# Batch 1's load order, the weights' gate, q(3)'s loads and the place of batch 2's attention in a fused attention and feed-forward kernel

## The chip, the cores and the metric

The kernel runs on one core of a Trainium2 chip. The metric is device time in microseconds (us) of one execution. A profile shows one execution under the hardware profiler; its span is 1.9 to 2.7 us shorter than the time of the run that it belongs to, so spans are compared with spans and times with times. PE is TensorE, PEld its loading of weights, ACT is ScalarE, DVE is VectorE, POOL is GpSimd, SP is SyncE. The granted clock is the share of full speed that PE was given, 1.00 or 0.50 in the stretches shown here. A trailing q, as in SPq, marks the issue of a DMA.

## The reference

Eight batches of eight heads, 576 positions of width 64, go through a linear attention. The result, 4608 tokens of width 512, goes through a gated feed-forward layer 512 to 1536 to 512.

```python
def phi(x, c, s):
    r = np.maximum(x, 0.0)
    return np.concatenate([r * c, r * s], axis=-1)
q_p, k_p = phi(q, cos_w, sin_w), phi(k, cos_w, sin_w)
kv  = np.einsum('bhsf,bhsd->bhfd', k_p, v)
z   = np.sum(k_p, axis=2)
num = np.einsum('bhsf,bhfd->bhsd', q_p, kv)
den = np.einsum('bhsf,bhf->bhs', q_p, z)[..., None] + 1e-06
x   = (num / den).transpose(0, 2, 1, 3).reshape(4608, 512)
g   = x @ w_gate
out = (0.5 * g * (1 + erf(g / sqrt(2))) * (x @ w_val)) @ w_out
```

## The kernel before

The 4608 tokens are cut into nine blocks of 512. Block n is multiplied by the gate and value weights in twelve units of eight matmuls (`gv_unit`, 512 columns, 1.73 us each); the second product is cut into parts of four matmuls (`o_part`, 0.86 us). A batch has 576 positions, so the attention of batch n+1 must be done, nearly, when block n+1 starts. It is woven into block n's units. Its steps are: load q, k, v in f32; prepare them in nine slices (`prep`: relu times cosine on DVE, relu times sine on ACT); transpose q (`turn_q`, two DMA transposes on the sync queue); `kv_unit`; five `nm_unit`, each eight small matmuls and a division on DVE; and transpose x (`turn_x` by DMA, `turn_x_pe` on PE with a copy on ACT). The argument takes each engine to run its instructions in the order of the program; two of the experiments below show it at work (ACT stood 2.79 and 7.45 us before sines whose load was late, with other work behind them: with the load order alone, and with q(3)'s loads behind).

The loads and the weights on GpSimd's queue, which the change reorders:

```python
nc.gpsimd.tensor_copy(gate, vx_tiles[0][:, 0, 0, 0:1])   # waits for v(0)'s cast; the weights come after it
load_w(0, 2)
load_w(2, 2)
for part in range(2):
    prep("q", 0, part, (8,), eng=nc.gpsimd)
for jt in (4, 6, 8, 10):
    load_w(jt, 2)
# ... q(1) in two halves
load_wo(0, 4)
# ... k(1) and v(1) in two halves each
load_wo(4, 4)
load_wo(8, 4)
# ... q(2), k(2), v(2), then the casts of v(1)
```

Between block 0 and block 1 stands a list `order`, in which the second product of block 0 (`o`) alternates with batch 1's attention. The loop over the blocks, cut to what the argument touches:

```python
for n in range(1, NB):
    b = n + 1
    t_kv, t_nm, t_q, t_k = {1: (4, 6, 7, 12), 2: (3, 4, 6, 9)}.get(n, (1, 2, 4, 8))
    for jt in range(JT):
        gv_unit(n, jt)
        # ...
        if n == 1 and jt == 0:
            turn_x(1, NT - 1)
            turn_q(b)
            loads(b + 1)              # q(3), k(3), v(3) on the sync queue
        # ...
        if jt == t_kv:
            kv_unit(b)
        # ... turn_x(b, i) for i = jt - t_nm - 1, casts of v
        if 0 <= jt - t_nm < NT:
            nm_unit(b, jt - t_nm)
        if b + 1 < B:
            if 0 <= jt - t_q < 3:
                prep_third("q", b + 1, jt - t_q)
            # ... k(b + 1) from unit t_k
            if jt == min(t_nm + NT, JT - 1):
                turn_q(b + 1)
                if b + 2 < B:
                    loads(b + 2)
```

## Time and profile before

| | before |
|---|---|
| time, median of the first 3 runs | 333.91 us (333.26 to 334.19) |
| span of the profile | 331.6 us |
| PE busy | 317.8 us, 96% |
| ACT, DVE busy | 48%, 51% |

The page of the kernel before gives the busy time of each engine, and then, in 40 slices of the span, the busy share of PE and its granted clock in tenths (9 is 90% or more).

```profile
PE 317.8 (96%) x2360; PEld 161.0 (49%) x2398; DVE 169.1 (51%) x400; ACT 159.8 (48%) x335; POOL 29.0 (9%) x45
...
PE   8799979989999999999999999999999999999995
...
PEclk9999989999999999999999999999999999999999
```

PE is the limit. Apart from the last slice, it has holes only in the first ten slices of 8.3 us, and the clock dips once, in the sixth. So only time before some 86 us can be had.

The view of the waits names the holes. Its columns are: the engine, tile and line that waited, what it waited for, the sum in us, how often, and the longest.

```profile
PE ps L401 <- DMA wo_sb<-in_moe_w_out_dram: 2.3, 1, 2.3
PE ps L281 <- DMA qT<-qp: 1.4, 1, 1.4
```

Line 401 is the second product, line 281 is `nm_unit`. The timeline of the kernel before shows where they stand: start, length, engine, line, operation, tiles, count, and in brackets the idle time before and what ended it.

```profile
44.29 1.03 PE L401 MATMUL ps<-wo_sb,hT 128*128 128x512 bf16 x4
...
47.62 1.86 PE L401 MATMUL ps<-wo_sb,hT 128*128 128x512 bf16 x4 [2.31 <-DMA wo_sb<-in_moe_w_out_dram]
...
60.17 1.02 PE L375 MATMUL ps<-xT,wg_sb 128*128 128x512 bf16 x4
...
63.13 8.26 SPq L192 DMA_TRANSPOSE qT<-qp  x2
...
73.63 0.19 PE L281 MATMUL ps<-kv_sb,qT 128*128 128x65 bf16 x1
...
75.25 0.40 PE L281 MATMUL ps<-kv_sb,qT 128*128 128x65 bf16 x7 [1.42 <-DMA qT<-qp]
```

The line at 60.17 is block 1's first unit. The four matmuls at 47.62 take 1.86 us, where the four at 44.29 take 1.03. The view by windows tells why. Its columns are the window, its length, then busy time and count for PE, PEld, DVE, ACT and POOL, the granted clock, the share of the DMA engines and GB/s.

```profile
44.02:47.44 3.42, 1.29 (x12) 0.66 (x10) 2.36 (x8) 1.64 (x3) 2.05 (x4) 1.00 1.24 212
47.44:50.85 3.41, 3.23 (x11) 1.41 (x11) 0.42 (x1) 0.00 (x0) 1.01 (x1) 0.50 1.08 373
```

PE stood still for 2.3 us, and then had 3.41 us at half clock. Half of that, 1.7 us, is the estimate of what it costs.

Last, the chain of waits that ended last holds two DMAs of this stretch (start, length, what):

```profile
32.07 15.52 DMA wo_sb<-in_moe_w_out_dram
...
66.56 8.64 DMA qT<-qp
```

### The profile page before, as it was taken

How to read it: one execution, taken by the hardware profiler on the slowest of the kernel's cores; microseconds unless marked ns; L12 is line 12 of the kernel's file. 1: busy time of each engine (PE TensorE's matmuls, PEld its weight loads, DVE VectorE, ACT ScalarE, POOL GpSimd, SP SyncE). 2: the span in 40 equal slices, each digit the busy share in tenths (PEclk: the TensorE clock that was granted, in tenths of full speed). 3: DMA queues.
4: the chain of work that ended last, by engine and by line, in shares of the span. 5: the costliest groups of instructions: out<-in, count | busy, mean ns of one | idle time of the engine just before them, and what ended most of it. 6: DMA issues, size and time to landing. Idle time of an engine off the chain costs nothing.

```text
span 331.6 us, 6186 instructions
## 1 busy us (share of the span) xinstructions
PE 317.8 (96%) x2360; PEld 161.0 (49%) x2398; DVE 169.1 (51%) x400; ACT 159.8 (48%) x335; POOL 29.0 (9%) x45
## 2 busy tenths in 40 slices
PE   8799979989999999999999999999999999999995
PEld 3585535545455445544554455445544444444443
DVE  5864654957846854755375537562632322223211
ACT  8764755947654752754365436553232223322220
POOL 1785350200000000000000000000000000000000
PEclk9999989999999999999999999999999999999999
DMA  7999999699599999979957994770321111111123
GB/s 283 215 177 266 299 283 348 133 153 381 93 156 367 160 134 355 219 115 183 389 96 113 198 370 79 126 128 12 79 57 39 44 43 35 32 34 32 32 65 95
DMA packets 67757, 53.23 MB, mean 161 GB/s; under 512 B 44048, under 2 KB 53008, under 8 KB 67728
## 3 DMA queue, kind: packets, MB, share of 16 engines
q1 hardware_dynamic: 57920, 40.91, 52.3%
q0 software_dynamic: 9648, 11.80, 15.8%
q8 instruction: 19, 0.31, 0.4%
q10 hardware_dynamic: 160, 0.13, 0.2%
q14 instruction: 10, 0.08, 0.1%
HBM read 37.75 MB, written 9.44 MB: 142 GB/s over the span
## 4 chain that ended last, share of the span: by engine, by line
PE 78%; DMA 13%; POOL 3%; ACT 2%; issue 1%; DVE 1%; SPq 0%; DVEq 0%
PE ps L375 46%; PE ps L401 26%; DMA wo_sb<-in_moe_w_out_dram 5%; DMA wv_sb<-in_moe_w_val_dram 3%; PE ps L281 3%; DMA qT<-qp 3%; PE ps L240 2%; DMA vf<-in_v_dram 2%; POOL wg_sb L94 1%; POOL wv_sb L95 1%; PE ps L624 1%; POOL qp L161 1%; ACT qp L159 1%; ACT gel L383 1%; ACT kp L159 0%
## 5 line engine op out<-in xcount | busy, mean ns | idle before, releaser
L384 DVE TENSOR_TENSOR hT<-gel,ps 128x512 bf16<-128x512 f32 (+2 forms) x114 | 75.0, 660 | 133.0 <-PE ps L375 131.7
L383 ACT ACTIVATE gel<-ps 128x512 f32<-128x512 f32 (+2 forms) x114 | 65.6, 575 | 112.0 <-PE ps L375 109.9
L375 PE MATMUL ps<-xT,wg_sb 128*128 128x512 bf16 (+2 forms) x451 | 111.5, 368 | 0.5
L375 PE MATMUL ps<-xT,wv_sb 128*128 128x512 bf16 (+2 forms) x445 | 110.5, 368 | 0.4
L401 PE MATMUL ps<-wo_sb,hT 128*128 128x512 bf16 x400 | 104.5, 383 | 3.7 <-DMA wo_sb<-in_moe_w_out_dram 2.3
L375 PEld LDWEIGHTS <-wv_sb 128*128 128x128 bf16 x456 | 44.0, 98 | 49.6 <-DMA wv_sb<-in_moe_w_val_dram 0.3
L375 PEld LDWEIGHTS <-wg_sb 128*128 128x128 bf16 x456 | 43.4, 98 | 47.4 <-issue 0.3
L401 PEld LDWEIGHTS <-hT 128*128 128x128 bf16 x420 | 38.7, 98 | 43.9 <-issue 3.7
L410 ACT COPY o_sb<-ps 128x512 f32<-128x512 f32 x34 | 20.0, 588 | 31.6 <-PE ps L401 30.5
L159 ACT ACTIVATE kp<-kf,sin_t 128x256 bf16<-128x256 f32 (+1 forms) x75 | 30.5, 483 | 0.3 <-DMA kf<-in_k_dram 0.3
L159 ACT ACTIVATE qp<-qf,sin_t 128x256 bf16<-128x256 f32 x70 | 30.4, 502 | 0.5 <-DMA qf<-in_q_dram 0.5
L294 DVE TENSOR_TENSOR x_sb<-ps,rec 128x512 bf16<-128x512 f32 x38 | 26.3, 691 | 1.3
L161 DVE TENSOR_SCALAR qp<-qf,cos_t 128x256 bf16<-128x256 f32 x71 | 22.4, 373 | 0.9 <-DMA qf<-in_q_dram 0.9
L281 PEld LDWEIGHTS <-qT 128*128 128x128 bf16 x304 | 14.5, 98 | 9.1 <-DMA qT<-qp 1.7
L161 DVE TENSOR_SCALAR kp<-kf,cos_t 128x256 bf16<-128x256 f32 x63 | 18.3, 349 | 0.0
L281 PE MATMUL ps<-kv_sb,qT 128*128 128x65 bf16 x304 | 16.1, 194 | 1.5 <-DMA qT<-qp 1.4
L249 ACT CAST kv_sb<-ps 128x260 bf16<-128x260 f32 x14 | 4.6, 382 | 16.1 <-PE ps L240 16.1
L139 PE MATMUL ps<-dummy 128*128 128x512 bf16 x28 | 9.1, 484 | 1.5 <-POOL dummy L113 1.5
L240 PEld LDWEIGHTS <-kp 64*128 64x128 bf16 x504 | 8.5, 95 | 3.1 <-issue 3.1
L178 DVE CAST vx<-vf 128x1152 bf16<-128x1152 f32 x12 | 9.2, 770 | 0.8 <-DMA vf<-in_v_dram 0.8
L240 PE MATMUL ps<-vx,kp 64*128 64x65 bf16 x504 | 9.3, 191 | 0.1
L292 DVE TENSOR_SCALAR den<-ps 128x8 f32<-128x8 f32 x38 | 6.1, 160 | 5.1 <-PE ps L281 5.0
(53 smaller groups left out, 96.1 us busy)
## 6 DMA issues: line engine op xcount, KB each, us to landing
out_dram<-o_sb SPq DMA_DIRECT2D x70, 128.0 KB, 2.6
kf<-in_k_dram SPq DMA_DIRECT2D x12, 576.0 KB, 6.8
vf<-in_v_dram SPq DMA_DIRECT2D x12, 576.0 KB, 8.6
qf<-in_q_dram SPq DMA_DIRECT2D x10, 576.0 KB, 5.1
qf<-in_q_dram POOLq DMA_DIRECT2D x4, 576.0 KB, 12.8
kf<-in_k_dram POOLq DMA_DIRECT2D x4, 576.0 KB, 13.9
vf<-in_v_dram POOLq DMA_DIRECT2D x4, 576.0 KB, 14.2
wg_sb<-in_moe_w_gate_dram POOLq DMA_DIRECT2D x6, 256.0 KB, 6.6
```

Of the source, the lines that this page charges most:

```text
L139: nc.tensor.matmul(bank(to), lhsT=dummy[:, 0:128], rhs=dummy, start=True, stop=True)
L159: nc.scalar.activation(o, i, AF.Relu, scale=tab[:, j:j + 1])
L161: (eng or nc.vector).tensor_scalar(o, i, 0.0, tab[:, j:j + 1], op0=ALU.max, op1=ALU.mult)
L178: copy(vx_tiles[b % 2][:, m0:m1, j0:j1, 0:D], staged["v", b][:, m0:m1, j0 * D:j1 * D].rearrange("p m (j d) -> p m j d", d=D),)
L240: nc.tensor.matmul(bank(6 + i)[:, m * (D + 1):(m + 1) * (D + 1)], lhsT=kp[rr, m, j, :], rhs=vx[rr, m, j, :], start=(j == 0), stop=(j == R ...
L281: nc.tensor.matmul(bank(b0 + h // 4)[:, (h % 4) * (D + 1):(h % 4 + 1) * (D + 1)], lhsT=q_cols(b, t, h), rhs=kv_sb[b][:, h // 2, h % 2, :], ...
L294: nc.vector.tensor_tensor(x, nm[:, :, :, 0:D], rec[:, :, :, None].to_broadcast([128, 2, 4, D]), op=ALU.mult,)
L375: nc.tensor.matmul(bank(b0 + g)[:, 0:w], lhsT=wt[:, ct, js], rhs=xt[:, ct, c0:c0 + w], start=(ct == 0), stop=(ct == CT - 1),)
L383: nc.scalar.activation(gel[:, 0:w], bank(b0)[:, 0:w], AF.Gelu)
L384: nc.vector.tensor_mul(hT[n][:, jt, c0:c0 + w], gel[:, 0:w], bank(b0 + 1)[:, 0:w])
L401: nc.tensor.matmul(bank(to), lhsT=hT[n][:, jt, tt * 128:(tt + 1) * 128], rhs=wo_sb[:, jt, :], start=(jt == 0), stop=(jt == JT - 1),)
L410: copy(o_sb, bank(to))
```

## The change

Its intent is to take those two waits away. The second part of `wo` goes ahead of v(1). The weights wait for an earlier event, so the whole queue runs ahead. q(2) is prepared sooner, piece by piece, between the pieces of batch 1's attention. q(3) loads before q(2)'s transposes, not behind them. Batch 2's attention starts at unit 7 of block 1, not 6, so that q(2) may arrive later. Transposes of x(0,4) go from DMA to PE. The diff, cut to its core (`...` marks cuts; left out are the move of k(2)'s slices by two units in block 1 and the new entries of `order`):

```diff
-    nc.gpsimd.tensor_copy(gate, vx_tiles[0][:, 0, 0, 0:1])
+    nc.gpsimd.tensor_copy(gate, phi["q", 0][:, 0, JA - 1, 0:1])
     load_w(0, 2)
     load_w(2, 2)
-    for part in range(2):
-        prep("q", 0, part, (8,), eng=nc.gpsimd)
     ...
     load_wo(0, 4)
-    for name in ("k", "v"): ... load(nc.gpsimd, name, 1, m, m + 2)
+    for m in (0, 2):
+        load(nc.gpsimd, "k", 1, m, m + 2)
     load_wo(4, 4)
+    for m in (0, 2):
+        load(nc.gpsimd, "v", 1, m, m + 2)
     load_wo(8, 4)
     # q(2), k(2); casts of v(1); and now v(2) behind the casts

     # block 0
+        if jt > 1:
+            prep("q", 0, jt - 2, (R - 1,), eng=nc.scalar)
-        if jt == 6:
-            turn_x(0, 4)
+        if jt == 7:
+            turn_x_pe(0, 4, 5, act_copy)
-        if jt == 10:          # q(1)'s first 16 transposes, now at the head of `order`
-            turn_j(1, 0, 2, range(4), 4, dve_copy)
-            turn_j(1, 2, 4, range(4), 5, act_copy)

     # `order`: q(2)'s slices 0 and 1, then 2, then 3 between the pieces;
     # nm(1, 4) and the transpose of x(1, 3) leave it for block 1
-    prep("q", 2, 0, range(R))
+    for m in (0, 2):
+        load(nc.sync, "q", 3, m, m + 2)

-        t_kv, t_nm, t_q, t_k = {1: (4, 6, 7, 12), 2: (3, 4, 6, 9)}.get(n, (1, 2, 4, 8))
+        t_kv, t_nm, t_q, t_k = {1: (5, 7, 7, 12), 2: (3, 5, 6, 9)}.get(n, (1, 2, 4, 8))
         for jt in range(JT):
-            gv_unit(n, jt)
+            if n > 1 or jt > 1:
+                gv_unit(n, jt)
+            else:
+                for i in range(2):
+                    gv_unit(n, i, jt * HALF, HALF)
+                    j = JA + 2 * jt + i
+                    prep("q", b, 1, (j,), eng=nc.scalar)
+                    prep("q", b, 0, (j,))
+                    if jt == i == 0:
+                        turn_x_pe(1, 3, 5, act_copy)
-                if n == 1 and jt == 0:
+                if n == 1 and jt == 2:
+                    prep("q", b, 0, (R - 1,))
+                    prep("q", b, 1, (R - 1,), eng=nc.scalar)
+                    turn_q(b)
+                    nm_unit(1, NT - 1)
+                if n == 1 and jt == 3:
                     turn_x(1, NT - 1)
-                    turn_q(b)
-                    loads(b + 1)
+                    loads(b + 1, ("k", "v"))
                     ...
                     if jt == min(t_nm + NT, JT - 1):
+                        if jt == t_nm + NT - 1:
+                            turn_x(b, NT - 1)
                         turn_q(b + 1)
```

## The prediction

> **What bounds the kernel.** TensorE: the page gives PE 317.8 of 331.6 us (96%), and the timeline shows a unit of the first feed-forward product (8 matmuls of 512 columns) every 1.73 us, nearly back to back, from 86 us to the end. Only PE stalls before 86 us can be won. Timeline and waits show them:
>
> 1. 45.15 to 47.62 us: PE waits for the second third of `wo_sb` (waits view: 2.3 us). GpSimd issued it behind k and v of batch 1; v1's halves landed at 43.12 and 45.20, `wo` at 47.58.
> 2. The windows view gives a granted clock of 0.50 from 47.44 to 50.85 us. [...] The loss is about 1.7 us.
> 3. 73.8 to 75.25 us: PE waits for q(2)'s DMA transposes (1.4 us) (63.13 to 75.20); q(3)'s loads, issued at 71.5, overlap their end.
> 4. 0.3 us at 20.6 us for `wv_sb`.
>
> Sum about 5.9 us: the most that can be had.
>
> **What the change does.**
> - `wo` ahead of v1: lands 3.6 us sooner (v1's share of the queue).
> - The gate moves from the v cast (10.53) to q's last cosine (9.38): weights start 1.1 us sooner and fill the DMA hole of 11.5 to 12.5 us. The removed GpSimd prep (2.6 us) and DMA transpose of x(0,4) let the queue run another 0.5 to 1 us ahead. I expect `wo` part two near 41.5 us, needed near 45: items 1, 2 and 4 vanish, 4.4 us.
> - Added on PE: four transposes (0.22 us). Halved units of block 1 cost nothing (0.44 us per 4+4 matmuls of 256 columns, half of 0.87). Sixteen transposes of q(1) only move.
> - New cost: q(2)'s preparation (0.4 us per slice on ACT, 0.3 on DVE) now sits inside batch 1's x chain. ACT must do q slices, output copies (0.59), x copies (0.59) and first gelus in order before the second halves of units 0 and 1 can start. Summed from q(2)'s landing (estimate 51 us), x(3) is copied near 58.6 us, while PE wants it near 57: 2 to 2.5 us of new PE stalls between 52 and 61 us.
> - q(2)'s transposes are then issued near 63.3 us, no sooner. Without q(3) behind them they take about 11, not 12.1 us, but PE reaches unit 7 near 72.3: the wait stays, about 2 us.
>
> **Sum.** Removed 4.4 + 1.4, added 0.2, new stalls 2.3 + 2.0[...]: gain about 2.5 us of 333.9. It gives half back.
>
> **Prediction.** 331.3 us; 8 in 10 between 328.8 and 333.9. Faster by over 2%: 0.04; within 2%: 0.95; slower: 0.01.
>
> **What would show it.** PE's wait on `wo_sb` gone; granted clock 1.0 from 10 to 320 us; PE on qT still 1 to 3 us, near 72 to 74; new PE idle at 56 to 60 us released by ACT's xT copies or DVE's hT; block 2's first unit near 83.5 us (before: 86.12); old pace after.
>
> **What would make it wrong.** If q(2) lands before 50 us, ACT is not late and the gain is 4 to 5 us. If earlier weights delay v and q of batch 0 (landed at 11.26 and 12.98), the start grows. [...]

The recorded sum came to a gain of about 2.5 us of 333.9. One term, a loss for a chance of another half clock, is cut from it, as no trace was named for it. The terms that are left give a gain of 1.3 us (4.4 + 1.4 less 0.2, 2.3 and 2.0), and with the one that is cut less still, so the 2.5 us do not follow from them; the record does not say what closes the gap. On the half clock, what the trace shows stands above: 3.41 us at 0.50, after 3.42 us with PE busy for 1.29.

## The result, and the profile after

| | before | after |
|---|---|---|
| time, median | 333.86 us in the same rounds | 331.94 us (4 runs, 331.39 to 332.48) |
| ratio, 95% interval | 1 | 0.9944 (0.9923 to 0.9966) |
| span of the profile | 331.6 us | 330.4 us |
| mean granted clock of the profile | 0.994 | 0.999 |

A ratio is the mean time of one kernel's fast runs over that of the other's of the same rounds, so it is not quite the ratio of the medians. The changed kernel ran six times more beside the experiments: 331.5 us, ratio 0.9931 (0.9909 to 0.9953). It gains about 2 us, well within 2%. All outputs are right.

The page of the kernel after:

```profile
PE 316.7 (96%) x2381; PEld 162.3 (49%) x2418; DVE 170.3 (52%) x402; ACT 161.1 (49%) x340; POOL 26.8 (8%) x43
...
PE   8899999979999997999999999999999999999995
...
PEclk9999999999999999999999999999999999999999
```

The dip of the clock is gone, and with it the hole of the sixth slice. The ninth slice (66 to 74 us), where PE waits for q(2), has gone from 8 to 7. And there is a hole where there was none, a 7 in the sixteenth slice (124 to 132 us). (The dip is gone in this profile, not in every run: the mean clock was 0.995 or less in 2 of the changed kernel's 10 runs of the result and the rerun, after 15 of 33 of the kernel before.) The waits of the kernel after say what it is:

```profile
PE ps L281 <- DMA qT<-qp: 3.7, 2, 1.9
```

No wait on `wo_sb` is left. The wait for a transposed q has become two waits, 3.7 us together instead of 1.4. The timeline of the kernel after shows the second product of block 0 running through (44.59), and both waits:

```profile
44.59 1.89 PE L401 MATMUL ps<-wo_sb,hT 128*128 128x512 bf16 x8
...
55.87 0.60 PE L375 MATMUL ps<-xT,wg_sb 128*128 128x256 bf16 x4
...
62.90 8.41 SPq L192 DMA_TRANSPOSE qT<-qp  x2
...
71.97 0.19 PE L281 MATMUL ps<-kv_sb,qT 128*128 128x65 bf16 x1
...
74.02 0.40 PE L281 MATMUL ps<-kv_sb,qT 128*128 128x65 bf16 x7 [1.86 <-DMA qT<-qp]
...
116.82 3.67 SPq L192 DMA_TRANSPOSE qT<-qp  x1
...
125.19 0.19 PE L281 MATMUL ps<-kv_sb,qT 128*128 128x65 bf16 x1
...
127.20 0.40 PE L281 MATMUL ps<-kv_sb,qT 128*128 128x65 bf16 x7 [1.82 <-DMA qT<-qp]
```

Before, the same transposes of q(4) were issued sooner and PE came later: they landed at 125.19 us, and after the change at 127.16, while PE came to them at 128.14 and 125.19. These two lines of the timeline before show that no wait stood there:

```profile
114.53 3.63 SPq L192 DMA_TRANSPOSE qT<-qp  x1
...
128.14 0.42 PE L281 MATMUL ps<-kv_sb,qT 128*128 128x65 bf16 x8
```

The chain of the kernel after holds the two transposes, and no `wo_sb`:

```profile
66.37 7.60 DMA qT<-qp
...
120.55 6.61 DMA qT<-qp
```

So the lead of the kernel after can be read at four points of the two traces:

| point | before | after | lead |
|---|---|---|---|
| value matmuls that wait for `wv_sb` in block 0 | 20.58 | 20.16 | 0.42 us |
| block 1's first unit | 60.17 | 55.87 | 4.30 us |
| block 2's first unit | 86.12 | 83.17 | 2.95 us |
| eight `nm_unit` matmuls of batch 4 released in full | 128.14 | 127.20 | 0.94 us |

The 4.30 us add up from the traces: 2.47 us of standing still and 1.67 us of half clock gone, 0.42 us from the start, and 0.48 us of work that moved into block 1; less 0.22 us of added transposes on PE and 0.49 us of a new wait at 33.07 us, where PE waits for the division behind x(0,4), which the change now transposes on PE. That makes 4.34. Block 1 takes 1.35 us of it back: the moved 0.48, a wait for q(2) that is 0.44 longer (1.86 for 1.42), and 0.43 that I have not itemised. Block 3 takes 2.0 us back with the wait for q(4). From there to the end the lead stays about that. (These losses are counted from start to start of matmuls; the idle times in brackets are up to 0.2 us shorter, as the ends of matmuls are modelled.)

The mean of the runs gives more than the two profiles, some 1.9 us instead of 1.2. A part of that may be the choice of the profiled runs, of which more below: the one after the change, 332.48 us, was the slowest of its four.

### The profile page after: what moved, and what is told of

Its sections match the earlier page's. It is cut to its first block, busy times and chain, and to the rows that moved or that the text cites. A ratio compares the mean times of both kernels' runs of the same rounds, so it can differ in the third digit from the quotient of the medians.

```text
span 330.4 us, 6242 instructions
## 1 busy us (share of the span) xinstructions
PE 316.7 (96%) x2381; PEld 162.3 (49%) x2418; DVE 170.3 (52%) x402; ACT 161.1 (49%) x340; POOL 26.8 (8%) x43
## 4 chain that ended last, share of the span: by engine, by line
PE 82%; DMA 8%; DVE 5%; issue 1%; ACT 1%; POOL 1%; SPq 1%; DVEq 0%; ACTq 0%
PE ps L375 51%; PE ps L401 24%; DMA qT<-qp 4%; PE ps L281 3%; DMA wv_sb<-in_moe_w_val_dram 2%; PE ps L240 2%; DVE kp L161 1%; DMA kf<-in_k_dram 1%; DVE kp L168 1%; DVE qp L161 1%; ACT kp L159 1%; PE ps L640 1%; PE ps L356 1%; POOL wg_sb L94 1%; SPq L192 1%
## 5 line engine op out<-in xcount | busy, mean ns | idle before, releaser
L401 PE MATMUL ps<-wo_sb,hT 128*128 128x512 bf16 x401 | 103.1, 379 | 1.4 <-issue 0.8
L375 PEld LDWEIGHTS <-wv_sb 128*128 128x128 bf16 x464 | 44.8, 98 | 49.3 <-DMA wv_sb<-in_moe_w_val_dram 0.7
L375 PEld LDWEIGHTS <-wg_sb 128*128 128x128 bf16 x464 | 44.1, 98 | 45.9
L159 ACT ACTIVATE qp<-qf,sin_t 128x256 bf16<-128x256 f32 x71 | 31.6, 502 | 2.6 <-DMA qT<-qp 2.1
L161 DVE TENSOR_SCALAR kp<-kf,cos_t 128x256 bf16<-128x256 f32 x63 | 20.0, 375 | 0.0
L360 ACT COPY xT<-ps 128x512 bf16<-128x512 bf16 (+1 forms) x13 | 7.0, 550 | 3.0 <-PE ps L356 2.9
## 6 DMA issues: line engine op xcount, KB each, us to landing
qf<-in_q_dram POOLq DMA_DIRECT2D x4, 576.0 KB, 12.1
```

Of the source, the lines that this page charges most:

```text
L159: nc.scalar.activation(o, i, AF.Relu, scale=tab[:, j:j + 1])
L161: (eng or nc.vector).tensor_scalar(o, i, 0.0, tab[:, j:j + 1], op0=ALU.max, op1=ALU.mult)
L375: nc.tensor.matmul(bank(b0 + g)[:, 0:w], lhsT=wt[:, ct, js], rhs=xt[:, ct, c0:c0 + w], start=(ct == 0), stop=(ct == CT - 1),)
L401: nc.tensor.matmul(bank(to), lhsT=hT[n][:, jt, tt * 128:(tt + 1) * 128], rhs=wo_sb[:, jt, :], start=(jt == 0), stop=(jt == JT - 1),)
```

## The experiments

One run is the changed kernel again; all others are edits of it or of the kernel before. They ran in three groups, each on one chip with its own runs of the kernel before (medians 333.83, 333.95 and 333.92 us). The group of the rerun (with the old kernel at 333.95) also has the whole units, q(3)'s loads behind and block 2 from unit 4, and only there does the changed kernel stand in the same rounds; elsewhere it is compared by the ratios to the kernel before. My theory at the start, on which A in the expectations builds from run to run, was: the load order removes the wait and the half clock; what then limits is when q(2)'s and q(4)'s transposes are issued; so the gain was there and was given back at these two. The rivals, under the further letters, differ from run to run; in the main they say that the spread-out preparation of q(2), or the earlier weights, costs or gains as much.

| kernel | median us | ratio to before (95%) |
|---|---|---|
| changed, again | 331.5 | 0.9931 (0.9909 to 0.9953) |
| load order alone | 333.02 | 0.9968 (0.9947 to 0.9989) |
| load order, and q(3)'s loads ahead | 332.32 | 0.9947 (0.9928 to 0.9965) |
| changed, old gate | 332.45 | 0.9959 (0.9939 to 0.9979) |
| changed, whole units | 332.88 | 0.9969 (0.9945 to 0.9993) |
| changed, q(3)'s loads behind | 336.71 | 1.0092 (1.0060 to 1.0124) |
| changed, block 2 from unit 4 | 332.43 | 0.9964 (0.9933 to 0.9995) |
| changed, slice 8 early | 331.05 | 0.9921 (0.9899 to 0.9944) |
| changed, q(4) turned early | 331.11 | 0.9919 (0.9896 to 0.9942) |
| changed, both of these | 329.46 | 0.9868 (0.9848 to 0.9888) |
| both, and x(0,4) a unit later | 329.2 | 0.9852 (0.9831 to 0.9873) |

### The changed kernel again

No edit. It is the reference for the group that it ran in.

> The changed kernel itself, unaltered, as the yardstick of this group on the same chip. All theories: near 331.9 us, a ratio of 0.993 to 0.996 to the kernel before; PE waits about 2 us on q(2)'s transposes near 72 us and up to 2 us on q(4)'s near 127 us.

It took 331.5 us (331.0 to 332.64). In this profile the wait for q(4) was 1.03 us, after 1.82 in the first. The transposes were issued at 114.17 and landed at 125.96, so 2.65 us sooner issued than in the first profile, and 1.20 sooner landed: the moment of issue alone does not set the landing.

### The load order alone

The kernel before, with nothing but the new order on GpSimd's queue (in short form, not the code):

```diff
-    k(1), v(1); load_wo(4, 4); load_wo(8, 4); q(2), k(2), v(2); casts of v(1)
+    k(1); load_wo(4, 4); v(1); load_wo(8, 4); q(2), k(2); casts of v(1); v(2)
```

> The kernel before with one part of the change: GpSimd's loads in the new order (second third of wo ahead of v of batch 1, v of batch 2 behind the casts of v). Gate, transposes and all of PE's order stay as before. Theory A (the later order of PE's work is needed to use the earlier wo): wo part two lands near 44.0 us (47.58 less v1's 3.58), PE's wait on it and the half-clock window vanish, but v of batch 1 now lands near 47.6 and its casts end near 48.8, so the kv products, which PE wants near 47.1, wait 1 to 2 us, and q(2)'s sines on ACT, which still wait for q(2) at 53.2, hold up the output copies. Block 1 starts 1.5 to 3 us sooner than before's 60.17, the wait on q(2)'s transposes stays, the time is 331.0 to 332.5 us. Theory B (the load order is the whole gain and the rest costs): 329.5 to 330.5. Theory C (useless alone, kv simply waits instead): 333.5 or more.

The wait on `wo_sb` and the half clock went, as theory A has it: the part landed at 43.67 us (before: 47.58). But only 0.8 us by the medians came of it: 333.02 us lies in none of the three ranges expected. A wait of the kv products for v(1), which A also expected, did not show. The waits of this run show what took their place:

```profile
PE ps L356 <- ACT o_sb L410: 1.8, 1, 1.8
PE ps L356 <- DVE x_sb L294: 1.4, 1, 1.4
```

The timeline of the same run shows the first of the two:

```profile
52.16 2.10 ACT L159 ACTIVATE qp<-qf,sin_t 128x256 bf16<-128x256 f32 x5 [2.79 <-DMA qf<-in_q_dram]
...
54.78 0.38 PE L356 MATMUL ps<-ident,x_sb 128*128 128x128 bf16 x4 [1.77 <-ACT o_sb L410]
```

PE is early now, and q(2) is not. ACT stands before q(2)'s first five sines until q(2) lands at 52.05. The copies of the outputs stand behind those sines, and PE stands 1.77 us before the `ps` that they free. In this trace ACT keeps the order of the program: it stood for 2.79 us, and the copies came at 54.17, behind the sines. So work behind a late load took up what the earlier `wo` had freed. The changed kernel, where q(2)'s slices are spread out, has neither of these two waits; but no run spreads the slices alone, and the next one gains more without it.

### The load order, and q(3)'s loads ahead

As the last one, and q(3) loads on the sync queue ahead of block 1 instead of behind q(2)'s transposes:

```diff
+    for m in (0, 2):
+        load(nc.sync, "q", 3, m, m + 2)
     ...
-            loads(b + 1)
+            loads(b + 1, ("k", "v"))
```

> The kernel before with two load edits only: GpSimd's loads in the new order (as in e1_load_order_only) and q(3)'s loads on the sync queue ahead of q(2)'s transposes. Theory A (e1's wait of 1.5 us at 80 us came from q(3) landing late: its slices stand in ACT's and DVE's order before the x tiles): that wait goes; but q(3)'s loads now share the DMA queues with q(2)'s transposes, which land later, and PE's wait near 72 us grows from 0.4 to about 1.5 us; time 332.3 to 333.0, little better than e1's 333.02. Theory B (these two edits are the whole change): 331.5 to 332.0.

It took 332.32 us (331.55 to 332.49), as theory A expected. (That the transposes of q(2) land later for sharing the DMA queues, as A has it, is not shown.) The wait of 1.38 us at 80.06, for an x behind q(3)'s slices, is gone; the one behind q(2)'s sines stays (1.79 us at 55.27), and PE waits 1.17 us for q(2) at 73.52. By the medians these two moves of loads together give 1.6 us, most of the 1.9 to 2.4 that the whole change gives, with q(2) prepared as in the kernel before. Against the load order alone (another group) the intervals overlap, so what q(3)'s loads add here is not settled.

### The changed kernel with the old gate

```diff
-    nc.gpsimd.tensor_copy(gate, phi["q", 0][:, 0, JA - 1, 0:1])
+    nc.gpsimd.tensor_copy(gate, vx_tiles[0][:, 0, 0, 0:1])
     load_w(0, 2)
     load_w(2, 2)
+    for part in range(2):
+        prep("q", 0, part, (8,), eng=nc.gpsimd)
     ...
-        if jt > 1:
-            prep("q", 0, jt - 2, (R - 1,), eng=nc.scalar)
```

> The changed kernel with the old gate (cast of v) and the two GpSimd preparations of slice 8 back in front of the third pair of weights. Theory A (the gate is worth only a small start): first-product units start 0.4 to 0.8 us later, wo part two lands 0.8 to 1.5 us later, near 42.5 to 43, still ahead of PE, q(2) lands near 51 instead of 49.97 and pushes ACT and DVE a little; time 0.4 to 1.2 us above the changed kernel, 332.3 to 333.1. Theory B (the earlier gate is what removes the wo wait): PE waits on wo again and the time goes back to 333.5 or more.

The second part of `wo` landed at 42.30 us and PE did not wait for it. So the gate is not needed against that wait. The median is 332.45 us; by the ratios it is 0.5 to 0.9 us slower than the changed kernel in its two sets of runs. The intervals overlap; the sign fits theory A, the size is not settled.

### The changed kernel with whole units

Block 1's first two units whole again, x(1,3) transposed ahead of the first.

```diff
+                if jt == 0:
+                    turn_x_pe(1, 3, 5, act_copy)
+                gv_unit(n, jt)
                 for i in range(2):
-                    gv_unit(n, i, jt * HALF, HALF)
                     j = JA + 2 * jt + i
```

> The changed kernel with units 0 and 1 of block 1 whole again (8 matmuls of 512 columns), the transposes of x(3) ahead of unit 0, and q(2)'s slices behind the units in the same order. Theory A (the halves let PE start 2 us before x(3) is copied, and that is why the stall of 2.3 us that I had predicted between 52 and 61 us did not come): PE waits about 1 us for x(3) and 1 us for its copy, first unit near 58 instead of 55.87 us, q(2)'s transposes issued about 1 us later, their wait falls to about 1.3 us, time about 1.0 us above the changed kernel. Theory B (halving is idle, since PE then only waits longer for q(2)'s transposes): time within 0.3 us.

The timeline of this run shows block 1's first unit, which needs x(1,3) in full:

```profile
56.93 1.02 PE L375 MATMUL ps<-xT,wg_sb 128*128 128x512 bf16 x4 [0.72 <-ACT xT L360]
```

The halves let PE start at 55.87 and hide the copy of x(1,3) behind 256 columns that do not need it. Whole units cost 1.4 us by the medians of the same rounds (332.88 after 331.5); the intervals overlap a little. Theory A expected about 1.0, but with a first unit near 58 us, and with a wait for q(2) fallen to 1.3; it was 1.77.

### The changed kernel with q(3)'s loads behind q(2)'s transposes

```diff
-    for m in (0, 2):
-        load(nc.sync, "q", 3, m, m + 2)
     ...
                     turn_q(b)
+                    loads(b + 1, ("q",))
```

> The changed kernel with q(3)'s two loads issued behind q(2)'s transposes again, as before. Theory A (of the prediction: loads that follow lengthen the transposes' end by about 1 us): q(2)'s transposes land 12 us after their first issue instead of 11.1, PE's wait near 72 us grows from 2.0 to about 3 us, time 0.7 to 1.2 us above the changed kernel. Theory B (the loads in front are what delays the transposes' start, or the order is indifferent): landing at or before 74.0 us, time within 0.3 us of the changed kernel or below it.

The prediction said that q(2)'s transposes take 12.1 us with q(3)'s loads behind them, and about 11 without. Without them they took 11.08 (62.90 to 73.98), but here, with the loads behind them again, they took 11.02 (62.40 to 73.42), and with the load order alone, where the loads are behind them too, 10.68 (61.42 to 72.10). In the other kernels with the loads ahead they took 10.59 to 11.52. So that reason is not borne out, though its number came true. Why they took 12.07 in the one profile of the kernel before stays open.

Yet the kernel lost 5.2 us against the changed one of the same rounds, its interval wholly above that of any other. Neither theory had that. The timeline of this run shows where:

```profile
78.85 1.30 ACT L159 ACTIVATE qp<-qf,sin_t 128x256 bf16<-128x256 f32 x3 [7.45 <-DMA qf<-in_q_dram]
...
82.45 0.61 PE L356 MATMUL ps<-ident,x_sb 128*128 128x128 bf16 x4 [4.65 <-DVE x_sb L294]
```

The same stretch in the view by windows of this run:

```profile
78.84:82.25 3.41, 0.00 (x0) 0.00 (x0) 2.40 (x7) 3.40 (x9) 0.00 (x0) 1.00 1.04 385
82.25:85.66 3.41, 3.21 (x18) 1.75 (x19) 3.28 (x11) 2.75 (x7) 0.00 (x0) 0.50 0.70 259
```

q(3)'s second half landed at 78.77 us. Its first slices come in unit 7 of block 1 (`t_q`), so ACT stood 7.45 us and DVE 3.82 us before them, and with them the gelus of block 1 (the next one came at 80.06) and the divisions of batch 2 (81.27), all behind them in the program. PE stood still for 4.65 us, and then got half clock for 3.41 us. In the changed kernel q(3) lands at 63.17. The early loads do not shorten the transposes (11.08 us with them, 11.02 here). They keep ACT and DVE from standing before a load.

### The changed kernel with block 2 from unit 4

```diff
-        ... 2: (3, 5, 6, 9)}.get(n, (1, 2, 4, 8))
+        ... 2: (3, 4, 6, 9)}.get(n, (1, 2, 4, 8))
```

> The changed kernel with block 2's attention starting at unit 4 as before, not at unit 5. Theory A (the shift only moved a wait): q(3)'s transposes land near 98.4 us while PE is at unit 4's end near 96.6, so PE waits 1.5 to 2 us there; q(4)'s transposes go out a unit earlier and the wait near 127 us is gone; time within 0.5 us of the changed kernel. Theory B (the shift to unit 5 was pure loss): no wait near 97 us, time 1.5 to 2 us lower. Theory C (it was worth its cost): time over 0.7 us higher.

With it q(4)'s transposes go back to unit 9 (issued at 113.07, landed at 123.47), and no wait for them is left. But batch 3's first `nm_unit` comes one unit sooner, and it needs q(3), whose transposes landed at 98.30. The timeline of this run:

```profile
96.49 0.19 PE L281 MATMUL ps<-kv_sb,qT 128*128 128x65 bf16 x1
...
98.34 0.40 PE L281 MATMUL ps<-kv_sb,qT 128*128 128x65 bf16 x7 [1.66 <-DMA qT<-qp]
```

The wait moved from block 3 to block 2. The time, 332.43 us with runs from 331.33 to 334.22, is 0.9 us above the changed kernel, which the intervals do not separate. Theory A had the waits right and the time within 0.5 us; by the median alone C would have it. So the shift to unit 5 was right for q(3) and wrong for q(4), and the two hang together only because the unit of q(4)'s transposes is computed from `t_nm`.

### The last slice of q(2) sooner

q(2)'s transposes wait for its ninth slice, which the change prepares behind unit 2. Here it goes behind unit 1:

```diff
+                if jt == 1:
+                    prep("q", b, 1, (R - 1,), eng=nc.scalar)
+                    prep("q", b, 0, (R - 1,))
     ...
                 if n == 1 and jt == 2:
-                    prep("q", b, 0, (R - 1,))
-                    prep("q", b, 1, (R - 1,), eng=nc.scalar)
                     turn_q(b)
```

> The changed kernel with the preparation of q(2)'s ninth slice moved ahead of unit 2 of block 1 on ACT and DVE (two statements moved). Theory A (q(2)'s transposes are late because their last slice stands behind unit 2's gelu and product on the in-order engines): transposes issued near 61.2 us instead of 62.90, landing near 72.3, PE's wait of 2.0 us at 72 to 74 shrinks to 0.3 to 0.6 us, the first unit of block 2 comes near 81.7 instead of 83.17; the second wait, at q(4)'s transposes at 127, stays; time 1.3 to 1.8 us below the changed kernel, about 330.3. Theory B (the transposes' end is set by DMA traffic, q(3)'s loads and stores in front of them): they land at 73.5 to 74 all the same and the time does not move.

(That engines run in order, which A takes for given, shows in two other runs, where ACT stood 2.79 and 7.45 us before a late load with work behind it.)

The issue moved from 62.90 to 61.91 us only (expected: 61.2), and the first one held the queue for 4.65 us, after 3.43. q(3)'s loads, under way until 63.2, could be the reason; but with whole units the first one took 4.61, and q(3) had landed at 62.70, before it was issued at 63.47. So why stays open. They landed at 73.21 (without this edit: 73.98, and 73.57 in the rerun), between A's 72.3 and B's 73.5, and PE waited 1.38 us for them. The median is 331.05 us, 0.4 to 0.9 below the changed kernel, where A expected 1.3 to 1.8. The profiled run was the slowest of the six (332.61) and has a wait of 2.7 us for q(4); the others lie between 330.68 and 331.42.

### q(4)'s transposes sooner

```diff
-                    if jt == min(t_nm + NT, JT - 1):
-                        if jt == t_nm + NT - 1:
+                    if jt == (9 if n == 2 else min(t_nm + NT, JT - 1)):
+                        if n == 1:
```

> The changed kernel with q(4)'s transposes (and the loads behind them) issued at unit 9 of block 2, straight behind the last product that reads q(3), and not at unit 10 behind the x transpose (3,4). Theory A (the wait of 2.0 us at 127 us in block 3 comes only from shifting block 2's attention from unit 4 to unit 5, which moved this issue one unit of 2.6 us later against PE): issue near 114.3 instead of 116.82, landing near 124.7, the wait at 127 is gone, time 1.7 to 2.1 us below the changed kernel, about 330.0. Theory B (contention with stores and loads makes these transposes slow): the wait stays over 1 us.

They were issued at 112.02 us and landed at 122.52. That is 4.80 us sooner issued, where a unit's 2.5 were expected, as the edit also puts them ahead of two stores and a transpose of x in the queue. One wait for a transposed q, that for q(2), is left in the waits of this run:

```profile
PE ps L281 <- DMA qT<-qp: 1.4, 1, 1.4
```

The wait at 127 us is gone, as theory A said. The size is not what it said: the median is 331.11 us, only 0.4 to 0.8 below the changed kernel, where 1.7 to 2.1 was expected. The wait at 127 us differs between the profiles of kernels that have it: 1.82 after the change, 1.03 when it ran again, and 1.40, 1.32 and 1.28 with the old gate, whole units and q(3)'s loads behind (there at 132 us). One profile had not told me that.

### Both, and x(0,4) a unit later

The last two edits together:

> The changed kernel with both repairs: q(2)'s ninth slice ahead of unit 2 of block 1, and q(4)'s transposes at unit 9 of block 2. Alone they took about 0.8 us each off (331.05 and 331.11 with a kernel before of 333.83, the changed kernel near 331.9). Theory A (two waits in two places, both in series with PE): the gains add, 330.0 to 330.6 us, wait near 72 us about 1.5 us, none near 127. Theory B (the second wait only passes on the first one's gain, so one repair is as good as both): 330.9 to 331.3.

329.46 us (329.19 to 330.24). The interval lies wholly below that of the changed kernel, and the median below the 330.0 to 330.6 that theory A expected of two gains that add. Of the waits for a transposed q one is left, 0.9 us for q(2). The two edits alone were too small to be told from noise by their times; together they are worth 2.1 us against the changed kernel's rerun, by the ratios 0.9931 and 0.9868.

Then, in block 0, x(0,4) goes to PE at unit 8 and not 7, so that PE does not wait for its division:

```diff
-        if jt == 7:
+        if jt == 8:
             turn_x_pe(0, 4, 5, act_copy)
```

> e5_both with the PE transposes of x(0,4) behind unit 8 of block 0 instead of unit 7, where PE waits 0.5 us for DVE's x. Theory A (that wait is in series): the 0.5 us at 33 us goes and the time is 0.2 to 0.5 us below e5_both. Theory B (PE then only waits longer for the casts of v of batch 1 near 48.6 us or for q(2)'s transposes): equal to e5_both within 0.2 us.

329.2 us (328.75 to 329.32), ratio 0.9852: 0.26 us below the last by the medians, with intervals that overlap, and the new wait of 0.5 us at 33 us is gone. This has the lowest median, 4.7 us below the kernel before in the same rounds. The view by windows of this kernel has PE busy all of the 44 us from 86 to 130:

```profile
86.00:130.00 44.00, 44.00 (x391) 22.10 (x390) 25.84 (x64) 23.35 (x51) 0.00 (x0) 1.00 1.05 235
```

In the kernel after, PE is busy 2.2 us less in the same window:

```profile
86.00:130.00 44.00, 41.81 (x363) 20.87 (x367) 25.06 (x63) 22.74 (x49) 0.00 (x0) 1.00 0.94 188
```

(The counts differ by more than the wait, as PE is further on in the program by then.)

### What could not be tried

The wait for q(2) is what is left. I wanted to split its two transposes into parts, so that the first `nm_unit` needs only the first; the forms that I tried did not build. So it stays open how low the wait can go.

## Why the prediction was right, and where it was not

The time was predicted as 331.3 us and is 331.94 and 331.5 in two sets of runs. But the sum holds two errors of about 2 us that cancel, so that the hit is in part luck.

- **The wait on `wo_sb`: right.** Predicted to land near 41.5 us, it landed at 41.61. The wait and the half clock went.
- **"Items 1, 2 and 4 vanish": wrong for item 4.** The wait for `wv_sb` was 0.3 us and is 0.4. The second pair of weights landed 0.42 us sooner, 20.11 for 20.53, and the matmuls behind it started as much sooner; but PE reached this point sooner too (its first unit at 16.91 for 17.71), and so it still waited.
- **New stalls of 2.3 us between 52 and 61 us: wrong.** They did not come. The failed step is "0.44 us per 4+4 matmuls of 256 columns". The timeline after shows that 0.44 is the step of four; a half unit of 4+4 takes 0.87:

```profile
56.96 0.40 PE L356 MATMUL ps<-ident,x_sb 128*128 128x128 bf16 x4
...
57.50 0.69 ACT L360 COPY xT<-ps 128x256 bf16<-128x256 bf16 x2
...
58.06 0.60 PE L375 MATMUL ps<-xT,wg_sb 128*128 128x256 bf16 x4
```

  PE has its own work until 58.06 us, not 57. The copy of x(1,3) has two pieces; the first, the one that block 1 needs, takes 0.41 us from 57.50 and ends at 57.91, and so PE does not wait. The copy was predicted for 58.6. So of the 2.3 us the cost of a half unit explains about 1.1 and the sooner copy 0.7; the prediction does not itemise the rest. q(2) also landed sooner, 48.46 and 49.97 for an estimate of 51. The prediction had named this case (before 50 us, ACT is not late and the gain is 4 to 5 us), and the lead at block 1 was 4.30. But q(2)'s landing is not what spared PE: ACT took up q(2)'s sines at 50.47, after a copy that had waited for PE, was done with them at 51.39, and stood 0.65 us until PE gave it an output to copy at 52.04.
- **A wait of about 2 us for q(2): right in size.** Issued at 62.90 (predicted 63.3), the transposes landed at 73.98, and PE waited 1.86 us. But the reason for 11 instead of 12.1 us is not borne out by the two runs with q(3)'s loads behind.
- **"Old pace after" block 2's first unit: wrong.** That unit came at 83.17 us (predicted 83.5). Then the wait for q(4) came, 2.0 us from 125.19 to 127.20. I had read the new tuples as a change to batch 3's attention alone, and not followed `t_nm + NT` to the transposes of q(4). This error of 2.0 us and the one of 2.3 us cancel by luck.
- **The half clock at 1.7 us: right in this trace, too large as an average.** Of the 33 runs of the kernel before beside the experiments, only 15 have a mean clock of 0.995 or less, as the profiled one has. In the three groups such runs are 0.65, 1.04 and 0.92 us longer than the others (334.28 to 333.63, 334.63 to 333.59, 334.42 to 333.50). This compares runs as they fell, and is no experiment. The 1.7 us were half of the 3.41 us at half clock; the trace agrees locally, with 1.67, but the runs as a whole differ by less. That later slack takes up the rest is argued and not shown. The spread of the runs also says why two profiles alone are a poor measure of this change.
- **The wait of 0.49 us at x(0,4): not predicted.** The transpose on PE was counted with 0.22 us of its own work, and not with the division that it now waits for.

"It gives half back" was the right form of the answer: of a lead of 4.30 us at block 1, 0.94 is left at 127 us in the two traces, which is more than half given back; the 1.9 and 2.4 us of the two sets of runs are nearer to half. What gives it back was named rightly for the wait for q(2), and missed for the other.

## What to carry to other kernels

When a schedule tuple moves, follow every place that reads it, the issue of transfers above all: a shift by one unit that was meant for one batch delayed the transposes of the next, and undoing this with one other edit nearly doubled the gain. ACT and DVE kept to the program's order here, and a late load held what stood behind its first user (2.79 us of ACT with the load order alone; 7.45 us of ACT and 3.82 of DVE with q(3)'s loads behind), so the place to look for the price of a load is the queue of ACT and DVE and not the DMA itself. And a prediction that hits the time can hold two errors of 2 us: check the points in between.

## What else the traces show of DMA transposes and of the half clock

- With only DMA transposes under way from 69 to 72 us (q's and, from 71.40, one of x), the DMA engines were fully busy (a share of 1.04) at 137 GB/s; from 76 to 82 us, loads ran at 345, with a share of 0.94. The windows of the kernel after show both:

```profile
69.00:72.00 3.00, 3.00 (x16) 1.33 (x14) 0.69 (x1) 1.45 (x3) 0.00 (x0) 1.00 1.04 137
76.00:82.00 6.00, 5.95 (x57) 3.40 (x57) 5.83 (x19) 5.06 (x11) 0.00 (x0) 1.00 0.94 345
```

- In the kernel before, a gap of PE of 2.3 us came before the half clock: a stretch of 3.42 us had PE busy for 1.29, and the next one, of 3.41 us, had half clock. With q(3)'s loads behind, one of 3.41 us with PE busy for 0.00 came before it, while one of 3.42 us with PE busy for 2.38 was followed by full clock. Perhaps the gap of the kernel before does not bring it in every run: only 15 of its 33 runs have a mean clock of 0.995 or less. The cause stays open; the 33 runs have no trace here that shows their gaps.
- The same pair of transposes, of one size, took from 10.33 us (q(4), after the change) to 12.45 us (q(3), in the same profile) from first issue to last landing. The cause stays open; for q(2), loads issued behind the transposes did not lengthen them (11.02 and 10.68 us with, 11.08 without).
